# The third group's work on k and its first use of q, moved from ahead of a gate product to behind it

## The chip, the cores and the metric

The kernel runs on one core of a Trainium2 chip. The metric is the device time of one execution in microseconds (us). TensorE (PE in the profile), VectorE (DVE), ScalarE (ACT) and GpSimd (POOL) each work through their own list of instructions in order and wait for each other by semaphores; SyncE (SP) issues the transfers.

## What is computed

Three stages follow each other on 8 batches of 576 tokens (4608 in all), 8 heads of 64 features:

```
q_s = softmax(q) over the 64 features of a head
k_s = softmax(k) over the 576 tokens of a batch
kv  = k_s^T v          # 64 x 64 per head
x   = q_s kv           # the attention's output, 512 features a token
xn  = x / rms(x) * rms_g
y   = (silu(xn w_gate) * (xn w_val)) w_out
z   = max(y w1, y w2, y w3) w_out2
```

Everything is float32 at the ends. The large products run as three matmuls on a high and a low part of each factor.

## The kernel before

The tokens are cut into nine **groups** of 512, g = 0 to 8. Groups 0 to 7 are the first 512 tokens of each batch, group 8 is the 64 left over of all eight. The work of the attention on one group falls into four **pairs of heads**, p = 0 to 3, and names carry both: k_2_0 is k of group 2 (the third), pair 0.

The first part of the kernel, up to about 620 us, is a loop `iteration(g, nxt, f)` over nine groups and f = 0 to 11, twelve blocks of 128 hidden features of the gated layer. Each call computes a **gate product** pg (twelve matmuls of 128x512, lines 640 to 642), ScalarE's tanh of it into t (L1003), VectorE's product with it (L1004), a **value product** pv (twelve more matmuls) and h (L1025). Between them stands the attention of a later group, spread over the calls so that TensorE need not stop. Even f and odd f make one *turn*; `turn_of` gives each target (g, p) a turn, and `due(n)` lists the targets whose turn is n turns ahead. For a target of group 2 or later the steps are:

- two turns ahead: k's columns come in, `k_max` takes the maximum per feature (km, L455), `q_exp` takes q's maximum and exponential by token (qm, L417; q, L429 and L430), and q's sums follow (L382 to L385). The statistics of q go to DRAM and come back as broadcasts (`spread_stats`, the tile stat).
- one turn ahead, odd f: `k_exp`. TensorE spreads km over the partitions by a transposition into the bank pb (L477), VectorE subtracts it from k (L478), ScalarE takes the exponential (L479).
- in its turn, even f, behind the gate product: `make_kv`. TensorE multiplies k and v into pk (L488, five matmuls in ten records); VectorE divides (L492 to L501) and the result is split into kvh and kvl.
- in its turn: `q_softmax` on the transposed q (qT: POOL L390, ACT L391, POOL L392), then `q_by_feature` (qh, ql).
- later: `make_x`. TensorE multiplies q and kv into px (L534 to L536), ScalarE copies it (xraw, L546) and squares it (sq, L552), GpSimd adds the squares up (sacc, L554). For group 2 this comes one turn later, at the head of an even f; for later groups two turns later.

When a group's four x are there, `token_rstd` sums the squares on TensorE (L590: pv of sacc or whole), and at the group's end the x are scaled (L622) and split into a high and a low part (ACT L99, DVE L100: xh, xl or x), which the next group's first gate product reads.

Beside this, ScalarE, VectorE and GpSimd recode the weights of the second layer (st, rooms_o, L247 to L274).

What is written here is not the order on the engines. The framework's scheduler places every instruction of each engine anew from the code's order and its dependencies, so that one moved call also moves neighbours that the diff does not name. TensorE's instructions stand in the order of its list, and one that waits holds back all behind it; the same goes for the other engines.

## Time and profile before

| | |
|---|---|
| median of 3 runs | 1506.61 us (1505.65 to 1508.04) |
| the profiled execution | 1505.86 us |
| its span, first to last instruction | 1504.1 us |
| TensorE busy | 1481.2 us, 98% of the span |
| VectorE busy | 1058.3 us, 70% |
| ScalarE busy | 607.1 us, 40% |
| GpSimd busy | 455.5 us, 30% |
| TensorE in the chain that ended last | 67% of the span; VectorE 3%, DMA 2% |

TensorE is the busiest by far, and its waits are few, so the profile is read by looking for the places where TensorE's list stood still. A row of the timeline gives the start of an instruction, its duration, engine, line, operation and tiles, and in brackets how long the engine had been idle and what ended that. Matmuls overlap: one follows the next after 0.23 us although each lasts 0.39 us. So time lost is read from start to start, and the idle time in brackets is less than what was lost.

### The profile page before, as it was taken

Reading aid. Unit: us, or ns where it says so; the run is one execution under the profiler, and the core shown is the slowest. Engines: PE = TensorE matmul, PEld = TensorE weight load, DVE = VectorE, ACT = ScalarE, POOL = GpSimd, SP = SyncE. Lnnn points to the kernel's source line nnn. Section 1 sums busy time; section 2 is a strip of 40 time slices with the busy share of each in tenths; the row PEclk is TensorE's granted clock in tenths of the full one; section 3 lists DMA queues with packets and bytes.
Section 4 is the critical chain, followed back from the end, with each engine's and each line's share of the span. In section 5 each row is a group of like instructions: output and inputs, shape, how many; then the busy total and the mean of one; then the engine's idle time right before and its main releaser. Section 6 shows DMA issues by size and latency. Waiting matters only on the chain.

```text
span 1504.1 us, 19788 instructions
## 1 busy us (share of the span) xinstructions
PE 1481.2 (98%) x6724; PEld 1215.4 (81%) x6724; DVE 1058.3 (70%) x1761; ACT 607.1 (40%) x1158; POOL 455.5 (30%) x383
## 2 busy tenths in 40 slices
PE   8899999999999999999999999999999999999998
PEld 5677878788888888888888888888888888888887
DVE  7998686867587864463798989658748748747622
ACT  6764443435343444332545545422422423413311
POOL 1002444444444444251365765111111111111100
PEclk9999999999999999999999999999999999999999
DMA  6868998878888968679535335265585585585572
GB/s 221 274 192 217 259 261 244 274 223 250 241 267 239 270 186 270 213 255 331 190 131 207 116 126 196 85 234 192 214 291 189 202 292 196 192 279 190 187 260 98
DMA packets 158757, 329.12 MB, mean 219 GB/s; under 512 B 31040, under 2 KB 55616, under 8 KB 158656
## 3 DMA queue, kind: packets, MB, share of 16 engines
q1 hardware_dynamic: 155200, 321.56, 66.4%
q10 hardware_dynamic: 3456, 6.29, 1.1%
q8 instruction: 53, 0.87, 0.2%
q14 instruction: 48, 0.39, 0.1%
HBM read 245.24 MB, written 82.55 MB: 218 GB/s over the span
## 4 chain that ended last, share of the span: by engine, by line
PE 67%; DVE 3%; DMA 2%; issue 1%; POOL 0%; ACT 0%; SPq 0%; DVEq 0%; ACTq 0%
PE p_a L647 4%; PE p_a L646 4%; PE p_a L648 4%; PE o_acc L647 4%; PE o_acc L646 4%; PE o_acc L648 4%; PE pv L642 3%; PE pv L640 3%; PE pv L641 3%; PE pg L640 3%; PE pg L641 3%; PE pg L642 3%; PE p_G L646 2%; PE p_G L647 2%; PE p_G L648 2%; PE o_a L646 2%
## 5 line engine op out<-in xcount | busy, mean ns | idle before, releaser
L1119 POOL TENSOR_TENSOR temps_wl<-temps_wl,temps_wh 128x512 f32<-128x512 f32 x36 | 48.2, 1339 | 348.5 <-ACT temps_wh L1118 273.8
L274 POOL TENSOR_TENSOR rooms_o<-st,rooms_o 128x256 fp32r<-128x256 f32 x77 | 62.6, 823 | 110.2 <-ACT rooms_o L273 99.7
L1004 DVE SCALAR_TENSOR_TENSOR t<-t,pg 128x512 f32<-128x512 f32 x64 | 43.8, 684 | 71.2 <-ACT t L1003 71.2
L1110 DVE TENSOR_TENSOR temps_wl<-temps_wl,p_a 128x512 f32<-128x512 f32 x72 | 49.2, 683 | 37.3 <-POOL temps_wl L1119 37.1
L429 POOL TENSOR_TENSOR q<-q,qm 128x512 f32<-128x512 f32 x30 | 34.3, 1145 | 135.5 <-DVE kr L494 82.2
L1114 ACT COPY temps_wh<-p_G 128x512 f32<-128x512 f32 x36 | 21.1, 586 | 106.0 <-PE p_G L648 105.8
L648 PE MATMUL p_a<-x_wh,chunk 128*128 128x512 f32 x160 | 62.3, 389 | 0.0
L647 PE MATMUL p_a<-x_wl,chunk 128*128 128x512 f32 x160 | 62.3, 389 | 0.0
L646 PE MATMUL p_a<-x_wh,chunk 128*128 128x512 f32 x160 | 62.3, 389 | 0.0
L646 PE MATMUL p_a<-x_wl,chunk 128*128 128x512 f32 x160 | 62.3, 389 | 0.0
L647 PE MATMUL p_a<-x_wh,chunk 128*128 128x512 f32 x160 | 62.3, 389 | 0.0
L648 PE MATMUL p_a<-x_wl,chunk 128*128 128x512 f32 x160 | 62.3, 389 | 0.0
L1025 DVE SCALAR_TENSOR_TENSOR h<-t,pv 128x512 f32<-128x512 f32 x66 | 45.2, 685 | 20.2 <-PE pv L642 18.4
L1116 DVE TENSOR_TENSOR temps_wl<-temps_wh,p_V 128x512 f32<-128x512 f32 x36 | 24.6, 684 | 43.9 <-PE p_V L648 43.9
L1003 ACT ACTIVATE t<-pg 128x512 f32<-128x512 f32 x64 | 37.8, 591 | 42.0 <-PE pg L642 38.3
L805 POOL TENSOR_TENSOR h_X<-h_Y,h_X 128x512 f32<-128x512 f32 x24 | 40.2, 1684 | 38.7 <-DVE o_xl L100 21.6
L809 POOL TENSOR_TENSOR h_Z<-h_Z,h_X 128x512 f32<-128x512 f32 x24 | 39.8, 1676 | 38.1 <-DVE h_X L802 34.2
L273 ACT CAST rooms_o<-st 128x256 fp32r<-128x256 f32 x77 | 31.5, 424 | 41.2 <-DMA w_dram<-rooms_o 21.6
L1004 DVE SCALAR_TENSOR_TENSOR rooms_o<-rooms_o,pg 128x512 f32<-128x512 f32 x42 | 28.7, 682 | 25.3 <-ACT rooms_o L1003 25.2
L807 POOL TENSOR_TENSOR h_Y<-h_W,h_Y 128x512 f32<-128x512 f32 x24 | 38.7, 1620 | 13.6 <-DMA h_W<-h_dram 12.9
L274 POOL TENSOR_TENSOR rooms_o<-rooms_o,rooms_o 128x256 fp32r<-128x256 f32 x36 | 28.8, 808 | 44.5 <-ACT rooms_o L273 36.8
L488 PEld LDWEIGHTS pk<-v,k 128*128 128x128 f32 x300 | 37.9, 190 | 5.0 <-ACT k L479 3.1
(1256 smaller groups left out, 4990.0 us busy)
## 6 DMA issues: line engine op xcount, KB each, us to landing
chunk<-w_dram SPq DMA_DIRECT2D x112, 768.0 KB, 4.4
w_dram<-rooms_o SPq DMA_DIRECT2D x113, 256.0 KB, 4.3
h_dram<-h SPq DMA_DIRECT2D x108, 256.0 KB, 4.2
stat<-stats SPq DMA_DIRECT2D x112, 128.0 KB, 5.1
words<-in_w SPq DMA_DIRECT2D x24, 512.0 KB, 6.9
chunk<-w_dram SPq DMA_DIRECT2D x48, 256.0 KB, 3.5
k<-in_k SPq DMA_DIRECT2D x30, 320.0 KB, 4.6
v<-in_v SPq DMA_DIRECT2D x30, 320.0 KB, 5.7
```

The source lines that it names most:

```text
L274: nc.gpsimd.tensor_sub(t[:, 1, :], src, t[:, 0, :].bitcast(F32))
L640: nc.tensor.matmul(pt, hi[:, j, s], xhs[kk], start=(kk == 0), stop=False)
L641: nc.tensor.matmul(pt, hi[:, j, s], xls[kk], start=False, stop=False)
L642: nc.tensor.matmul(pt, lo[:, j, s], xhs[kk], start=False, stop=(kk == 3))
L646: nc.tensor.matmul(pt, ah, bh, start=first, stop=False, skip_group_check=onto)
L647: nc.tensor.matmul(pt, ah, bl, start=False, stop=False, skip_group_check=onto)
L648: nc.tensor.matmul(pt, al, bh, start=False, stop=last, skip_group_check=onto)
L805: nc.gpsimd.tensor_sub(x, y, x)
L1004: nc.vector.scalar_tensor_tensor(t, t, 1.0, pg, op0=ALU.add, op1=ALU.mult)
L1025: lows.append(nc.vector.scalar_tensor_tensor(h, t, 0.5, pv, op0=ALU.mult, op1=ALU.mult))
L1110: nc.vector.tensor_add(y, x, pt)
L1119: nc.gpsimd.tensor_add(w, u2, s5)
```

## The change

Two steps are moved inside `iteration`. For targets of group 2 and later, `k_exp` no longer stands ahead of the odd gate product but behind it and its tanh. For targets of group 2, `make_x` no longer stands ahead of the even gate product but behind it, just ahead of `make_kv`. Nothing is added, nothing removed: 24 calls of `k_exp` and 4 of `make_x` move. (Group 8 has no k of its own, and group 1 has its own calls, which stay.)

```diff
@@ -941,8 +941,6 @@
             for t in due(-1):
                 if t[0] > BY_FEATURE:
                     q_by_feature(*t)
-                else:
-                    make_x(*t)
             for t in due(0):
                 q_softmax(*t)
             for t in due(1):
@@ -966,8 +964,6 @@
                     for t in due(2):
                         k_max(*t)
                         q_stats(*t)
-            for t in due(1):
-                k_exp(*t)
             for t in due(0):
                 if t[0] == BY_FEATURE:
                     q_by_feature(*t)
@@ -1003,8 +999,14 @@
         nc.scalar.activation(t, pg, AF.Tanh, scale=0.5)
         nc.vector.scalar_tensor_tensor(t, t, 1.0, pg, op0=ALU.add, op1=ALU.mult)
         if not odd:
+            for item in due(-1):
+                if item[0] == BY_FEATURE:
+                    make_x(*item)
             for item in due(0):
                 make_kv(*item)
+        else:
+            for item in due(1):
+                k_exp(*item)
         if nxt == BY_FEATURE and f == 10:
             spread_rstd(nxt)
             for p in range(4):
```

On TensorE the built program differs in just these moves and one more. All 24 transpositions of km stand behind the twelve matmuls of the gate product, and px of the third group behind the even gate product. SyncE's list is the same to the last row. On VectorE, ScalarE and GpSimd the neighbours of the moved instructions change places too. Three places matter below. In the changed kernel lines from 1003 on have numbers two to four away: the tanh is L999 there, the product with it L1000, h L1027.

The first place is the change from the first group to the second (g = 1, f = 0). ScalarE's list there, before:

```order
L99 CAST x_1_2_1396<-xraw_1_3_1223 128x512
L479 ACTIVATE k_2_0_1229<-k_2_0_1229 128x640
L391 ACTIVATE qT_2_0_1304<-qT_2_0_1304 128x512
L1003 ACTIVATE t_1_0_1460<-pg_1_0_1447 128x512
L99 CAST qh_2_0_1521<-qT_2_0_1304 128x512
```

And in the changed kernel:

```order
L99 CAST x_1_2_1392<-xraw_1_3_1223 128x512
L391 ACTIVATE qT_2_0_1304<-qT_2_0_1304 128x512
L479 ACTIVATE k_2_0_1229<-k_2_0_1229 128x640
L999 ACTIVATE t_1_0_1460<-pg_1_0_1447 128x512
L99 CAST qh_2_0_1517<-qT_2_0_1304 128x512
```

The exponential of k for (2, 0) has moved behind that of the transposed q of the same target. TensorE's list there in the changed kernel, from the last matmul of the gate product:

```order
L642 MATMUL pg_1_0_1447<-x_1_2_1392,wl_(1, 0)_519 128x512
L640 MATMUL pv_1_0_1479<-x_1_0_1384,wh_(1, 0)_516 128x512
L641 MATMUL pv_1_0_1479<-x_1_0_1384,wh_(1, 0)_516 128x512
L642 MATMUL pv_1_0_1479<-x_1_0_1384,wl_(1, 0)_519 128x512
L488 MATMUL pk_2_0_1463<-v_0_0_219,k_2_0_1229 128x129 x5
L640 MATMUL pv_1_0_1479<-x_1_0_1384,wh_(1, 0)_516 128x512
```

Before, pk of (2, 0) stood right behind the gate product; now three matmuls of the value product stand ahead of it.

The second place is the last x of the third group (g = 1, f = 8). ScalarE before:

```order
L546 ACTIVATE xraw_2_3_1980<-px_2_3_1976,gain_214 128x512
L552 ACTIVATE sq_2_3_1982<-px_2_3_1976 128x512
L273 CAST rooms_o5_1430<-rooms_o7_1432 128x256
L1003 ACTIVATE t_1_8_2011<-pg_1_8_1998 128x512
L430 ACTIVATE q_3_2_1858<-q_3_2_1858 128x512
L247 ACTIVATE st2_4_1911<-st2_4_1911 128x512
```

And in the changed kernel:

```order
L273 CAST rooms_o5_1430<-rooms_o7_1432 128x256
L999 ACTIVATE t_1_8_2002<-pg_1_8_1989 128x512
L546 ACTIVATE xraw_2_3_2009<-px_2_3_2005,gain_214 128x512
L430 ACTIVATE q_3_2_1849<-q_3_2_1849 128x512
L552 ACTIVATE sq_2_3_2011<-px_2_3_2005 128x512
L247 ACTIVATE st2_4_1911<-st2_4_1911 128x512
```

The last square of the group, which the sum of squares needs, has moved behind an exponential of q. On GpSimd the addition of it (L554) has moved in the same way behind the subtraction that this exponential waits for (L429).

The third place is VectorE's list at (6, 2), g = 4, f = 11. Before:

```order
L382 TENSOR_REDUCE qs_6_3_4490<-q_6_3_4277 128x8
L478 TENSOR_TENSOR k_6_2_4343<-k_6_2_4343,pb_6_2_4495 128x640
L383 TENSOR_SCALAR qs_6_3_4490<-qs_6_3_4490 128x8
L248 TENSOR_SCALAR st2_19_4392<-st2_19_4392 128x512
L385 RECIPROCAL qr_6_3_4493<-qs_6_3_4490 128x8
L249 SCALAR_TENSOR_TENSOR st2_19_4392<-st2_19_4392 128x512
L261 TENSOR_TENSOR st2_19_4392<-st2_19_4392 128x256
L1004 SCALAR_TENSOR_TENSOR rooms_o6_1431<-rooms_o6_1431,pg_4_11_4510 128x512
```

And in the changed kernel:

```order
L382 TENSOR_REDUCE qs_6_3_4490<-q_6_3_4277 128x8
L383 TENSOR_SCALAR qs_6_3_4490<-qs_6_3_4490 128x8
L248 TENSOR_SCALAR st2_19_4392<-st2_19_4392 128x512
L385 RECIPROCAL qr_6_3_4493<-qs_6_3_4490 128x8
L249 SCALAR_TENSOR_TENSOR st2_19_4392<-st2_19_4392 128x512
L261 TENSOR_TENSOR st2_19_4392<-st2_19_4392 128x256
L478 TENSOR_TENSOR k_6_2_4343<-k_6_2_4343,pb_6_2_4521 128x640
L1000 SCALAR_TENSOR_TENSOR rooms_o6_1431<-rooms_o6_1431,pg_4_11_4506 128x512
```

The subtraction from k stands five instructions later. At the change to the next group, (2, 0), (3, 2) and (7, 2), it stands behind the four splits of x (L100) and, there too, behind the product with the tanh.

## Rows read from the trace of the kernel before

**Rows 1.** The page: busy time by engine; TensorE's granted clock in 40 slices.

```profile
PE 1481.2 (98%) x6724; PEld 1215.4 (81%) x6724; DVE 1058.3 (70%) x1761; ACT 607.1 (40%) x1158; POOL 455.5 (30%) x383
...
PEclk9999999999999999999999999999999999999999
```

**Rows 2.** Timeline, TensorE, first gate product of the second group (start, duration, instruction, [idle]).

```profile
120.87 0.39 PE L640 MATMUL pg<-x,wh_(1, 0)_516 128*128 128x512 f32 x1
121.96 0.50 PE L641 MATMUL pg<-x,wh_(1, 0)_516 128*128 128x512 f32 x1 [0.70 <-DVE x L100]
...
124.62 1.28 PE L488 MATMUL pk<-v,k 128*128 128x129 f32 x10
```

**Rows 3.** Timeline there, GpSimd and ScalarE.

```profile
124.95 1.27 POOL L390 TENSOR_TENSOR qT<-qT,stat 128x512 f32<-128x512 f32 x1 [13.20 <-DMA stat<-stats]
...
126.25 0.63 ACT L391 ACTIVATE qT<-qT 128x512 f32<-128x512 f32 x1 [4.26 <-POOL qT L390]
126.79 0.58 ACT L1003 ACTIVATE t<-pg 128x512 f32<-128x512 f32 x1
```

**Rows 4.** Timeline, TensorE, px of (2, 1).

```profile
146.77 0.39 PE L642 MATMUL pv<-x,wl_(1, 3)_770 128*128 128x512 f32 x1
147.96 0.49 PE L534 MATMUL px<-qh,kvh 128*128 128x512 f32 x1 [0.80 <-ACT qh L99]
...
149.25 0.39 PE L640 MATMUL pg<-x,wh_(1, 4)_815 128*128 128x512 f32 x1
```

**Rows 5.** Timeline, ScalarE, GpSimd, TensorE, around the last square of the third group.

```profile
177.63 0.59 ACT L552 ACTIVATE sq<-px 128x512 f32<-128x512 f32 x1
...
181.38 0.63 ACT L430 ACTIVATE q<-q 128x512 f32<-128x512 f32 x1 [2.35 <-POOL q L429]
181.92 0.65 ACT L247 ACTIVATE st<-st 128x512 f32<-128x512 f32 x1
...
178.36 1.29 POOL L554 TENSOR_TENSOR sacc<-sacc,sq 128x512 f32<-128x512 f32 x1 [0.34 <-ACT sq L552]
...
181.81 0.84 PE L590 MATMUL pv<-ones_f,sacc 128*128 128x1 f32 x7
```

**Rows 6.** Timeline, TensorE, first gate product of the third group, from its first matmul to pk.

```profile
201.82 0.40 PE L640 MATMUL pg<-xh,wh_(1, 0)_516 128*128 128x512 f32 x1
...
205.71 0.50 PE L488 MATMUL pk<-v,k 128*128 128x129 f32 x3
```

**Rows 7.** Timeline, TensorE, transposition of km of (4, 3), and what stands ahead of it.

```profile
283.67 0.39 PE L642 MATMUL pv<-x,wl_(1, 0)_519 128*128 128x512 f32 x1
285.49 0.30 PE L477 MATMUL pb<-ident,km 128*128 128x128 f32 x1 [1.43 <-DVE km L455]
```

**Rows 8.** Timeline, TensorE, sum of squares of the sixth group.

```profile
396.73 0.49 PE L590 MATMUL pv<-ones_f,whole 128*128 128x1 f32 x3 [0.52 <-POOL whole L558]
```

**Rows 9.** Timeline, VectorE, ScalarE, TensorE, around k of (6, 2).

```profile
429.00 0.81 DVE L478 TENSOR_TENSOR k<-k,pb 128x640 f32<-128x640 f32 x1
429.72 0.17 DVE L383 TENSOR_SCALAR qs<-qs 128x8 f32<-128x8 f32 x1
...
431.39 0.68 DVE L1004 SCALAR_TENSOR_TENSOR rooms_o<-rooms_o,pg 128x512 f32<-128x512 f32 x1
...
429.90 0.74 ACT L479 ACTIVATE k<-k 128x640 f32<-128x640 f32 x1 [2.18 <-DVE qs L383]
...
429.68 0.39 PE L640 MATMUL pg<-x,wh_(1, 0)_516 128*128 128x512 f32 x1
...
431.04 0.83 PE L488 MATMUL pk<-v,k 128*128 128x129 f32 x6
```

**Rows 10.** Timeline, TensorE and VectorE, around k of (7, 2).

```profile
504.66 0.39 PE L640 MATMUL pg<-xh,wh_(1, 0)_516 128*128 128x512 f32 x1
...
506.09 0.61 PE L488 MATMUL pk<-v,k 128*128 128x129 f32 x4
...
505.39 0.67 DVE L1004 SCALAR_TENSOR_TENSOR rooms_o<-rooms_o,pg 128x512 f32<-128x512 f32 x1
```

## The prediction

> **What bounds the kernel now.** The page comes first: TensorE is busy 98% of the span, the next engine 70% [rows 1]. So the time is the length of TensorE's list plus the places where it stands still, and the change adds no instruction to any list. The timeline of TensorE comes next, read from start to start in the part that the change touches (115 to 575 us). Undisturbed, six matmuls of 512 columns take 1.36 us, from 429.68 to 431.04, so one follows the next after 0.23 us [rows 9]; three of them cost 0.69, twelve 2.74. Every start that is later than that is lost. Then the other engines' timelines show what came late. In this part the list stands still for half a microsecond or more at only six places [rows 2, 4, 6, 7, 8 and 10]. They are the first gate products of three groups, where a split of x is late; px of (2, 1), where qh and ql are late; one transposition of km; and one sum of squares.
>
> **What the moves take away.** I call the sum of what is gained and lost so far the *shift*; TensorE carries it to the end, for it is the bound in all that follows.
>
> 1. px of (2, 1). From the last matmul of a product at 146.77 to the first of the next at 149.25, four steps that should take 0.92 took 2.48 [rows 4]: 1.55 lost, on ScalarE's qh and then VectorE's ql. Behind the gate product px comes 2.74 later, and both are there. **-1.55.** The other three px had no such wait.
> 2. The transposition of km for (4, 3) came 1.82 after the matmul before it, instead of 0.23, because km was late [rows 7]. Behind the gate product it comes 2.74 later and km is there. **-1.6.**
> 3. Where the third group begins, the twelve matmuls of the gate product took from 201.82 to 205.71, 3.89 for 2.74 [rows 6]: 1.15 lost on the splits of x, which had stood behind the subtraction from k on VectorE. That subtraction (0.81 [rows 9]) now stands behind the splits. The splits come earlier and TensorE later, so this goes. In its place pk of (3, 2) may wait, for its subtraction now comes last. By rows that are not this late it waits for nothing; at most it takes 0.8 back. I take 0.1: **-1.0** (-1.1 to -0.3).
>
> **What the moves put in their place.** Four things are new or larger.
>
> 4. (2, 0), where the second group begins. On ScalarE the exponential of k now stands behind that of qT. That one started at 126.25 because it waited for GpSimd, which had been idle 13.2 us until the broadcast of the statistics landed [rows 3]. The transfers' list is the same, so it starts then again. The next on ScalarE began at 126.79; k's exponential, 0.74 long [rows 9], then ends at 127.53. TensorE follows a late input after 0.05 (the split that began at 121.22 and ended at 121.91 let it start at 121.96 [rows 2]), and a matmul after a wait costs 0.1 more (that product took 3.75 from 120.87 to pk at 124.62, 1.0 over, of which 0.86 before the late matmul and the rest behind it [rows 2]). So pk begins at 127.58 and is 0.1 longer. Before it began at 124.62, with three matmuls fewer ahead of it (0.69), which are no loss: 127.68 - 124.62 - 0.69 = **+2.4**. The wait for x at 121.96 goes, but that is in this number: TensorE just stands about 3.3 us at pk instead.
> 5. The last square of the third group now stands on ScalarE behind the exponential of q for (3, 2), which began at 181.38 and let the next start at 181.92 [rows 5]. With the square's 0.59 it ends at 182.51, GpSimd starts 0.14 later (178.36 after a square that ended at 178.22) and adds for 1.29: 183.94, and the sum of squares on TensorE begins at 183.99. TensorE comes there at 181.81, less 0.1 for the transposition that now stands behind, plus a shift of 2.4 - 1.55 = 0.85, so at 182.56. The wait is 1.4 and the 0.1 behind it. That is the low end. q's exponential hangs on q's maximum on VectorE, which stands behind h and now behind the moved subtraction of (3, 0), and h is released by TensorE; if that chain moves with the shift it is 2.4. I take **+2.3**, near the high end, because the subtraction is in that chain as well.
> 6. (6, 2). k's exponential ended at 430.64, 0.40 before TensorE came to pk at 431.04 [rows 9]. The subtraction moves behind the five instructions that took from 429.72 to 431.39, 1.67 in all [rows 9]. So the exponential ends at 432.31 and pk starts at 432.36, 1.32 late, and 0.1 behind it: **+1.4**. If VectorE does not move with the shift, as little as 0.9.
> 7. (7, 2). The splits lost TensorE 0.74 (1.43 for three steps of 0.23 [rows 10]). They come earlier, and the subtraction stands behind them and behind the product with the tanh. That product began at 505.39 [rows 10]; without the subtraction ahead of it 0.72 earlier, at 504.67, for the next instruction on VectorE starts 0.72 after a subtraction of 0.81, 0.09 before its end [rows 9]. By the same 0.09 the subtraction follows the product (0.67 long) after 0.58. It ends at 506.06, the exponential some 0.8 later, and pk starts at 506.9 instead of 506.09, with 0.1 behind it: **+0.9**. If VectorE lags less than the shift, the whole wait is hidden and the place gains 0.7.
> 8. The sum of squares of the sixth group waits for GpSimd at 396.73 [rows 8]. The transposition ahead of it, 0.1, lay within that wait and now stands behind it, and GpSimd moves a little with the shift: **+0.25** (0.1 to 0.4).
>
> The other 20 calls of k's step and three of x's cost nothing that I can price: TensorE did not wait for their results, and the move takes 2.74 of TensorE's time and a few instructions of VectorE's. That cover is thinner after the change, and it is a rival below.
>
> **The sum**: -1.55 - 1.6 - 1.0 + 2.4 + 2.3 + 1.4 + 0.9 + 0.25 = +3.1. The profiled execution took 1505.86; with the change I expect 1509.0. The median of the runs is 0.75 above the profiled one, so the median I expect is **1509.7**, 0.2% above 1506.61. With all low ends the sum is about 0, with all high ends 4.2. A measurement of this kernel tells about 0.2%, 3.0 us, from no change, so my forecast lies on that line.
>
> **The rivals.**
> - *Not slower: ScalarE and VectorE arrive in time.* Steps 5, 6 and 7 all hang on one thing, how far VectorE and ScalarE lag behind TensorE. If they come to the moved instruction some 1.5 us earlier against TensorE than these rows say, which they would if they do not share the shift, those waits close. Then 2.3, 1.4 and 1.6 go from the sum: -2.2, a median of 1504.4. For it: the products with the tanh and the splits lose the subtraction ahead of them. Against it: it takes all three at once, and at (6, 2) only 0.40 was left [rows 9].
> - *More waits at pk.* The move uses up most of the cover of other products of k and v. Two of them coming 0.6 late give 4.3 and a median of 1510.9. For it: VectorE is at 70% and the lag grows with what stands ahead. Against it: at no other place does the subtraction move behind as much as at a group's end.
> - *TensorE's clock falls at the new wait.* The granted clock stayed at its full level all through, beside waits on TensorE of up to 1.4 us in the part in question [rows 1, 7]; at (2, 0) there would be one of 3.3. At the lower level (1.2 of 2.4 GHz) a step would take 0.46 instead of 0.23; for the nine matmuls left of that product that is 2.1 more, a median of 1511.8. The Trainium skill bears on it (TensorE: Matmul & The Clock Gate, section Why this matters for your kernels): it advises against pauses of TensorE between bursts of matmuls, because an idle stretch can bring the clock back to half. The rows here have no wait as long as the new one, so they neither bear it out nor deny it.
>
> That the change does not do what it says is no rival: the order of the built program shows it.
>
> **How the numbers follow.** The forecast, 0 to +4.2, has 0.74; it lies on both sides of the line, 0.36 within 0.2% and 0.38 above. The first rival has 0.12, half of it beyond 0.2%, if the other low ends come too, and half within. More waits have 0.08 and the clock 0.06, all slower by more. That makes 0.06 faster, 0.42 the same, 0.52 slower. The range reaches from 1506.4, a little under the forecast's low end, to 1512.2, over the last two rivals' prices; below it lies most of the first rival.
>
> **What would show it.** The timeline of TensorE at the first gate product of the second group: pk some 3.3 us late with ScalarE's k named, and no wait for x at the starts of the second, third and seventh groups. px of (2, 1) and the transposition of (4, 3) without idle time. The sum of squares at g = 1, f = 9 late with GpSimd's sacc named, some 2.3. pk of (6, 2) and (7, 2) 1.3 to 1.6 late. I am wrong if pk of (2, 0) starts without a wait (then step 4 falls and the sum is below 1), or if the waits taken away come back at the same matmuls.

## The result and the profile after

The changed kernel took 1513.3 us (median of 6 runs, 1511.17 to 1514.97) where the kernel before took 1505.87 (6 runs, 1502.68 to 1508.04): a ratio of 1.0053, with a 95% interval of 1.0042 to 1.0064. The profiled execution took 1511.17, its span 1509.4. So it is slower, and by more than the range of the prediction allowed: of the 7.4 us the forecast had 3.1.

The page first, against [rows 1]: TensorE's busy time rose by 2.6 us though it has the same list, and the span by 5.3. Of the 2.6, 1.2 lie ahead of 115 us, where TensorE's list is the same: there the granted clock was at half from 48.6 to 52.0.

```profile
span 1509.4 us, 19787 instructions
...
PE 1483.8 (98%) x6724; PEld 1218.1 (81%) x6724; DVE 1061.8 (70%) x1761; ACT 609.0 (40%) x1158; POOL 455.3 (30%) x383
```

The same chain as in [rows 2] and [rows 3]: the timeline of TensorE at the second group's first products, then of GpSimd and ScalarE there.

```profile
124.12 0.39 PE L642 MATMUL pv<-x,wl_(1, 0)_519 128*128 128x512 f32 x1
127.07 2.52 PE L488 MATMUL pk<-v,k 128*128 128x129 f32 x10 [2.56 <-ACT k L479]
...
131.99 0.39 PE L640 MATMUL pg<-x,wh_(1, 1)_581 128*128 128x512 f32 x1
...
124.46 1.27 POOL L390 TENSOR_TENSOR qT<-qT,stat 128x512 f32<-128x512 f32 x1 [13.10 <-DMA stat<-stats]
...
125.76 0.63 ACT L391 ACTIVATE qT<-qT 128x512 f32<-128x512 f32 x1 [5.01 <-POOL qT L390]
126.30 0.72 ACT L479 ACTIVATE k<-k 128x640 f32<-128x640 f32 x1
```

This is the new wait as forecast: k's exponential starts when that of qT lets it, and pk follows it. pk starts 2.95 after the matmul ahead of it, 2.72 late; forecast were 3.3, the broadcast landed 0.5 sooner. But pk's ten records now last 2.52 where the kernel before needed 1.28 [rows 2]. The table by stretches says why (columns: stretch, its length, busy time of PE, PEld, DVE, ACT and POOL, then the granted clock, DMA share, GB/s):

```profile
126.00:128.00 2.00, 0.93 (x4) 0.94 (x5) 0.47 (x1) 1.73 (x4) 1.53 (x2) 0.77 0.32 86
128.00:130.00 2.00, 2.00 (x10) 1.91 (x9) 1.41 (x4) 1.02 (x2) 0.74 (x1) 0.50 0.61 149
130.00:132.00 2.00, 2.00 (x10) 1.60 (x9) 0.86 (x3) 0.30 (x1) 0.00 (x0) 0.87 1.03 377
132.00:134.00 2.00, 2.00 (x10) 1.68 (x9) 1.81 (x3) 0.00 (x0) 0.00 (x0) 1.00 1.04 424
```

From about 127.1 to 130.5 TensorE ran at the lower of its two levels, 1.2 instead of 2.4 GHz. The whole place, from the first gate matmul to the first of the next gate product, took 11.47 us (120.52 to 131.99), against 7.66 before (120.87 to 128.53): 3.81 more. From pk to the next gate product an undisturbed list needs 3.23 (before, 124.62 to 128.53, less three matmuls of 0.23); here it took 4.92. So 1.69 of the 3.81 is the clock, and 2.12 the wait.

px of (2, 1) and the transposition of (4, 3), [rows 4] and [rows 7], now come without idle time (timeline of TensorE):

```profile
153.16 0.40 PE L534 MATMUL px<-qh,kvh 128*128 128x512 f32 x1
...
292.18 0.39 PE L642 MATMUL pg<-x,wl_(1, 1)_601 128*128 128x512 f32 x1
292.40 0.27 PE L477 MATMUL pb<-ident,km 128*128 128x128 f32 x1
```

The sum of squares of the third group, [rows 5]: TensorE, then ScalarE, then GpSimd.

```profile
183.23 0.39 PE L642 MATMUL pv<-x,wl_(1, 8)_1135 128*128 128x512 f32 x1
185.84 1.05 PE L590 MATMUL pv<-ones_f,sacc 128*128 128x1 f32 x8 [2.22 <-POOL sacc L554]
...
183.25 0.63 ACT L430 ACTIVATE q<-q 128x512 f32<-128x512 f32 x1 [1.43 <-POOL q L429]
183.79 0.58 ACT L552 ACTIVATE sq<-px 128x512 f32<-128x512 f32 x1
...
184.51 1.27 POOL L554 TENSOR_TENSOR sacc<-sacc,sq 128x512 f32<-128x512 f32 x1 [1.29 <-ACT sq L552]
```

As forecast, the square stands behind q's exponential, and the sum is 2.4 late. The third group's start, [rows 6], is what went against the forecast (TensorE, VectorE, ScalarE):

```profile
205.77 0.39 PE L640 MATMUL pg<-xh,wh_(1, 0)_516 128*128 128x512 f32 x1
...
208.41 0.50 PE L641 MATMUL pg<-xl,wh_(1, 0)_516 128*128 128x512 f32 x1 [0.16 <-DVE xl L100]
208.74 0.40 PE L642 MATMUL pg<-xh,wl_(1, 0)_519 128*128 128x512 f32 x1
210.50 1.38 PE L488 MATMUL pk<-v,k 128*128 128x129 f32 x10 [1.37 <-ACT k L479]
...
208.28 0.68 DVE L1000 SCALAR_TENSOR_TENSOR rooms_o<-rooms_o,pg 128x512 f32<-128x512 f32 x1
208.88 0.81 DVE L478 TENSOR_TENSOR k<-k,pb 128x640 f32<-128x640 f32 x1
...
209.72 0.74 ACT L479 ACTIVATE k<-k 128x640 f32<-128x640 f32 x1 [4.74 <-DVE k L478]
```

The gate product is slowed by little, 0.33 at 208.41, but pk waits 1.53 for product, subtraction and exponential one after the other. The remaining places, [rows 8 to 10] and two more (TensorE):

```profile
285.71 0.49 PE L488 MATMUL pk<-v,k 128*128 128x129 f32 x2 [0.56 <-ACT k L479]
...
400.88 1.05 PE L590 MATMUL pv<-ones_f,whole 128*128 128x1 f32 x8 [0.22 <-POOL whole L558]
...
436.90 1.38 PE L488 MATMUL pk<-v,k 128*128 128x129 f32 x10 [1.41 <-ACT k L479]
...
511.34 1.28 PE L488 MATMUL pk<-v,k 128*128 128x129 f32 x10
```

pk of (4, 2) waits, which the sum did not have (it was a rival); pk of (6, 2) waits 1.57, as forecast; pk of (7, 2) does not wait, against the forecast.

*Lateness* below is how much later the same product begins than in the first trace of the kernel before, and a place's price is how much the lateness grows across it. Every variant below has the trace of one execution, which can lie some us from its median. The first trace of the changed kernel gives:

| place | forecast | measured |
|---|---|---|
| ahead of 120 us | 0 | -0.35 |
| start of the second group, (2,0) | +2.4 | +3.81 |
| px of (2,1) | -1.55 | -1.60 |
| sum of squares, third group | +2.3 | +2.35 |
| start of the third group, (3,2) | -1.0 | +0.95 |
| pk of (4,2), then transposition of (4,3) | 0, -1.6 | +0.83, -1.67 |
| pk of (5,2) | 0 | +0.35 |
| sum of squares, sixth group | +0.25 | -0.27 |
| (6,2) | +1.4 | +1.61 |
| (7,2) | +0.9 | -0.74 |
| rest | 0 | 0 |
| sum | +3.1 | +5.3 |

### The profile page after: what moved, and what is told of

The parts are those of the page before. It is cut to its first block, busy times and chain, and to the rows that moved or that the text cites. A ratio compares the mean times of both kernels' runs of the same rounds, so it can differ in the third digit from the quotient of the medians.

```text
span 1509.4 us, 19787 instructions
## 1 busy us (share of the span) xinstructions
PE 1483.8 (98%) x6724; PEld 1218.1 (81%) x6724; DVE 1061.8 (70%) x1761; ACT 609.0 (40%) x1158; POOL 455.3 (30%) x383
## 4 chain that ended last, share of the span: by engine, by line
PE 66%; DVE 5%; DMA 2%; issue 1%; POOL 1%; ACT 1%; SPq 0%; DVEq 0%; POOLq 0%; ACTq 0%
PE p_a L646 4%; PE p_a L648 4%; PE p_a L647 4%; PE o_acc L648 3%; PE o_acc L647 3%; PE o_acc L646 3%; PE pv L642 3%; PE pv L640 3%; PE pv L641 3%; PE pg L640 3%; PE pg L641 3%; PE pg L642 3%; PE p_G L646 2%; PE p_G L648 2%; PE p_G L647 2%; PE o_a L646 2%
## 5 line engine op out<-in xcount | busy, mean ns | idle before, releaser
L274 POOL TENSOR_TENSOR rooms_o<-st,rooms_o 128x256 fp32r<-128x256 f32 x77 | 62.5, 820 | 116.4 <-ACT rooms_o L273 101.8
L1000 DVE SCALAR_TENSOR_TENSOR t<-t,pg 128x512 f32<-128x512 f32 x64 | 43.8, 685 | 72.7 <-ACT t L999 72.5
L429 POOL TENSOR_TENSOR q<-q,qm 128x512 f32<-128x512 f32 x30 | 34.6, 1154 | 134.6 <-DVE kr L494 81.7
L1027 DVE SCALAR_TENSOR_TENSOR h<-t,pv 128x512 f32<-128x512 f32 x66 | 45.2, 685 | 19.6 <-PE pv L642 18.0
L999 ACT ACTIVATE t<-pg 128x512 f32<-128x512 f32 x64 | 37.9, 592 | 42.8 <-PE pg L642 37.6
L488 PE MATMUL pk<-v,k 128*128 128x129 f32 x300 | 41.5, 286 | 8.0 <-ACT k L479 7.9
L999 ACT ACTIVATE rooms_o<-pg 128x512 f32<-128x512 f32 x42 | 24.9, 593 | 52.9 <-PE pg L642 52.8
L274 POOL TENSOR_TENSOR rooms_o<-rooms_o,rooms_o 128x256 fp32r<-128x256 f32 x36 | 28.9, 811 | 49.9 <-ACT rooms_o L273 47.6
```

The lines of the kernel that those rows point to most:

```text
L274: nc.gpsimd.tensor_sub(t[:, 1, :], src, t[:, 0, :].bitcast(F32))
L488: nc.tensor.matmul(pk[:, 0 : P + 1], k_t[g, p][:, c, :], v_t[g, p][:, c, :], start=(c == 0), stop=(c == 4))
L999: nc.scalar.activation(t, pg, AF.Tanh, scale=0.5)
L1027: lows.append(nc.vector.scalar_tensor_tensor(h, t, 0.5, pv, op0=ALU.mult, op1=ALU.mult))
```

## The experiments

**The theory** at the start: the waits are where the forecast put them, the lower clock behind the longest adds 1.7, and each place's price stands by itself. **The rivals**: that the clock does not hang on the wait; and that waits are not added up but passed on, since what comes late hangs on broadcasts, GpSimd and VectorE rather than on TensorE, so that time saved at one place is waited for at the next.

Most variants use the same edit, which lets one choose the calls that move. The changed kernel has all 24 in the first list and all four of group 2 in the second.

```diff
+            for t in due(1):
+                if t not in K_BEHIND:
+                    k_exp(*t)
...
             for item in due(1):
-                k_exp(*item)
+                if item in K_BEHIND:
+                    k_exp(*item)
```

and the same for `make_x` with X_BEHIND. Each variant ran beside the kernel before on the same chip, and each ratio is to that; chips differ, the medians of the kernel before were 1508.8 to 1509.5 on these.

### The changed kernel once more

> The changed kernel once more. Theory (waits plus clock): TensorE stands some 2.6 us at the product with k of (2, 0) and the granted clock falls to 0.5 behind it, which makes the second group's start 3.8 us longer than before; the time is 1511 to 1515, 0.5% above before. The executions of the changed kernel that took up to 3.8 us longer than its profiled one have further stretches at the lower clock, behind the 2.2 us wait for the sum of squares or in the first stage near 49 us. Rival: the clock is at half in no second place of the later stages, and the spread of executions comes from the first stage alone (before 115 us), as it does in the kernel before.

1518.57 us (5 runs, 1517.91 to 1519.91), the kernel before 1509.53 (17 runs): 1.0060 (1.0043 to 1.0078). The timeline of GpSimd and of TensorE, and the granted clock (columns as above) at (2,0) and at (6,2):

```profile
126.66 1.26 POOL L390 TENSOR_TENSOR qT<-qT,stat 128x512 f32<-128x512 f32 x1 [14.26 <-DMA stat<-stats]
...
129.27 0.49 PE L488 MATMUL pk<-v,k 128*128 128x129 f32 x2 [4.15 <-ACT k L479]
...
440.60 2.52 PE L488 MATMUL pk<-v,k 128*128 128x129 f32 x10 [2.28 <-ACT k L479]
...
130.00:132.00 2.00, 2.00 (x9) 1.86 (x9) 1.73 (x5) 1.22 (x2) 0.94 (x1) 0.50 1.01 343
440.00:442.00 2.00, 1.40 (x6) 1.40 (x7) 2.00 (x6) 1.42 (x4) 0.31 (x1) 0.58 1.04 376
442.00:444.00 2.00, 2.00 (x10) 1.76 (x8) 1.14 (x2) 2.00 (x5) 1.13 (x2) 0.56 0.98 204
```

The broadcast landed 5.1 after the gate product's start (121.56) instead of 3.9, and the wait at (2,0) is 4.15 instead of 2.56: that place costs 4.95 here. (6,2) costs 3.98 instead of 1.61, half clock included, (7,2) costs +0.84, near the forecast's +0.9, and pk of (6,1) 0.97. So the rival, that no second place of the later stages has the lower clock, is wrong: (6,2) has one. The places of the theory, the sum of squares or the first stage, are not those of this trace: its first stage shows full clock. The first trace of the changed kernel was at the fast end of what the kernel does; this one shows where the rest of the 7.4 can lie, but the other executions have no trace.

### One part alone

> Only k's step is moved; x's products stay ahead of the gate products. Theory: the second group's start loses 3.8 as in the changed kernel (2.1 wait, 1.7 clock); the sum of squares of the third group is not late, because its last square is ahead of q's exponential again (0 instead of +2.35); the third group's start, (4,3), (5,2), (6,2) and (7,2) are as in the changed kernel (+1.0, -0.85, +0.35, +1.7, -0.75 and -0.3 for the sixth group's sum of squares); px of (2,1) waits 1.55 as before: in all +5.0, 1511 us. Rival: the new shift of 3.8 covers the wait at px of (2,1) as well, since its inputs hang on a broadcast that is not late: +3.4, 1509.

```diff
+    K_BEHIND = [(g, p) for g in range(2, 8) for p in range(4)]
+    X_BEHIND = []
```

1517.97 (1.0052, 1.0035 to 1.0069). The lateness, 0.97 at the second group's start, grew by 4.0 there, and px of (2,1) gained 1.55 although x is not moved: the rival on that point is right. The sum of squares is not late (-0.1), as expected. But the third group's start cost 3.3 where 1.0 was expected: the gate product now waits at all four splits (2.36 in all), and pk another 1.54. The total, 8.4 us above the kernel before, is past both expectations and cannot be told from the changed kernel's on this chip, 1518.57: leaving x's products where they were saved nothing.

> Only x's product of the third group is moved; k's step stays ahead of the gate products. Theory: px of (2,1) loses its wait (-1.6) and the sum of squares of the third group is 2.3 late, because its last square stands behind q's exponential: +0.7, 1506.6 us, and no stretch at the lower clock at the second group's start. Rival: the sum of squares is late only as far as the second group's start is (the chain hangs on TensorE): then 1.4 here and -0.2 in all, 1505.7.

```diff
+    K_BEHIND = []
+    X_BEHIND = [(2, 0), (2, 1), (2, 2), (2, 3)]
```

1511.73 (11 runs; 1.0014, 1.0002 to 1.0025). px gained 1.60, the sum of squares waited 2.60 for GpSimd, and the clock was at half from 182.9 to 189.7: the place cost 5.8. The third group's start then gained 1.15, for TensorE came so late that x was there. Both expectations had the sum of squares right in kind and too small, and neither had a fall of the clock.

### The clock or the wait

> The changed kernel with eleven matmuls of 512 columns more (2.5 us, their result is overwritten) on TensorE ahead of the product with k of (2, 0), where it stands idle 2.6 us. Theory (the idle time lets the clock fall): no stretch at 0.5 near 127 to 131 us, the product with k starts at the same time as without them, and the next gate product begins 1.7 us earlier: 1.8 instead of 3.5 later than in the kernel before; the whole 1.7 shorter than the changed kernel, some 1511.6 where that takes 1513.3. Rival (the idle time is not the cause; it is the transfers or the place in the program): the clock falls all the same and the gate product begins 3.5 later.

```diff
+            if g == 1 and f == 0:
+                pv = bank("V", f"pv_{g}_{f}")
+                for _ in range(11):
+                    nc.tensor.matmul(pv, wh[wkey][:, 1, 0:P], xhs[0], start=True, stop=True)
+                third = product_in(pv, wh[wkey], wl[wkey], 1, xhs, xls, 0, 1)
+                with tc.issue_after(third.ins):
+                    for item in due(0):
+                        make_kv(*item)
+                product_in(pv, wh[wkey], wl[wkey], 1, xhs, xls, 1, 4)
```

The timeline of TensorE and its granted clock at (2,0):

```profile
126.94 1.38 PE L488 MATMUL pk<-v,k 128*128 128x129 f32 x10 [0.35 <-ACT k L479]
...
126.00:128.00 2.00, 1.65 (x12) 1.22 (x11) 0.59 (x1) 1.73 (x4) 1.66 (x2) 1.00 0.22 36
128.00:130.00 2.00, 2.00 (x11) 1.67 (x11) 1.71 (x6) 0.90 (x2) 0.62 (x1) 1.00 0.70 188
```

pk starts when k's exponential lets it, as without the fill, and the clock stays at full level; from pk to the next gate product 3.29 instead of 4.92. That is the price of the clock again, 1.63: the idle time is the cause there, and the rival falls (one trace with the fill, against six without it in which the clock fell here). The next gate product begins 1.70 later than in the first trace of the kernel before (1.8 expected), of which 1.23 had been gained ahead of the place; the place costs 2.93, against 3.81 and 4.95 in the two traces of the changed kernel. The whole did not get shorter, though: 1520.49 (1.0071, 1.0053 to 1.0088). The eleven instructions made the scheduler place others differently in the second group, and TensorE waited 2.57 at 167.5 and 3.84 at 186.2 for k's exponential, there with the lower clock from 182.8 to 189.6. As a test of the total it says nothing, as one of the place it does.

### Taking single places back

> The kernel before once more, for a second trace of it beside those of the other variants. Theory (the places of the waits belong to the order of the instructions, their sizes partly to when the statistics' broadcasts land): TensorE stands still at the same six places as in the first trace, each within 0.7 us of it, no stretch at the lower clock between 100 and 620 us, and a time within 0.3% of 1506. Rival (the chip's state makes the waits): waits at other places, or a stretch at half clock between 100 and 620 us.

1507.99 us. Only three of the six places lose half a microsecond or more as before: the starts of the second and third groups, and the sum of squares of the sixth group, which waited 1.07 instead of 0.56. px of (2,1) lost 0.74 instead of 1.55, the transposition of (4,3) 0.30 instead of 1.59, the seventh group's start 0.22 instead of 0.74; the transposition of (3,2) waited 0.85 instead of 0.27. And the clock was at half from 400.0 to 403.4 without any change to the kernel, which cost 1.6: here the rival is right. So part of the waits and of the clock belongs to the single execution, and one trace against one trace tells a place's price to about 1.3 us, a fall of the clock apart.

> The changed kernel, but k's step of (2,0) stays where it was. Theory: the wait at the product with k of (2,0) and the half clock behind it go (-3.8 to -5), the wait for x at 121 comes back inside that; of the rest the sum of squares of the third group stays late, by more than in the changed kernel since TensorE comes earlier: +3.5 on before, ratio 1.0023. Rival: all later waits hang on broadcasts and not on TensorE, so what is saved is waited for at the sum of squares and at (3,2) and (6,2): ratio 1.005, as the changed kernel.

```diff
+    K_BEHIND = [(g, p) for g in range(2, 8) for p in range(4) if (g, p) != (2, 0)]
```

1519.77 (6 runs; 1.0074, 1.0057 to 1.0091): no gain at all. The wait at (2,0) and the fall of the clock at 127 are gone, and the lateness at 128.5 is 0.01. Then, in the timeline of TensorE, the next three pk and the sum of squares wait:

```profile
151.27 1.38 PE L490 MATMUL pk<-v,k 128*128 128x129 f32 x10 [0.70 <-ACT k L481]
...
165.96 1.38 PE L490 MATMUL pk<-v,k 128*128 128x129 f32 x10 [1.53 <-ACT k L481]
...
179.91 1.38 PE L490 MATMUL pk<-v,k 128*128 128x129 f32 x10 [0.79 <-ACT k L481]
...
186.74 1.05 PE L592 MATMUL pv<-ones_f,sacc 128*128 128x1 f32 x8 [2.70 <-POOL sacc L556]
```

With the lower clock from 189.0 to 192.5 the lateness is 6.8 at 194.9, more than in either trace of the changed kernel (4.3 and 6.0). The rival is right: the wait at (2,0) had covered these.

> The changed kernel, but x's product of (2,3) stays ahead of the gate product, so that its square stands ahead of q's exponential on ScalarE. Theory: the sum of squares of the third group is not late: 2.3 less than the changed kernel, ratio 1.004 on before; the third group's start is unchanged (its splits and k's subtraction hang on VectorE). Rival: the sum of squares waits all the same, since what makes it late is the shift of 3.8 ahead of it: ratio 1.0055.

```diff
+    X_BEHIND = [(2, 0), (2, 1), (2, 2)]
```

1518.24 (6 runs; 1.0070, 1.0053 to 1.0087). The last square stands ahead of q's exponential again, and the sum of squares is on time (+0.2): step 5 of the prediction named the right cause. The 2.35 are not saved, however. The gate product of the third group, reached sooner, waits 2.3 for the four splits and pk 1.54, with the lower clock behind it: 4.8 there instead of 0.95. The first of the splits and pk (TensorE; lines have other numbers here):

```profile
205.36 0.50 PE L643 MATMUL pg<-xl,wh_(1, 0)_516 128*128 128x512 f32 x1 [0.50 <-DVE xl L100]
...
211.52 0.98 PE L490 MATMUL pk<-v,k 128*128 128x129 f32 x6 [1.37 <-ACT k L481]
```

Theory and rival were both wrong on the total: the wait went, and moved on.

> The changed kernel, but k's step of (3,2), (4,2), (5,2), (6,2) and (7,2), the five that stand at a group's start, stays where it was. Theory (each of these stands on VectorE behind the splits and the product with the tanh, and TensorE waits for it at the product with k): their waits go, 5 to 7 us together in the traces of the changed kernel; what is left is the second group's start (+4 to +5), px of (2,1) (-1.6), the sum of squares (+2) and (4,3) (-1.65): +3.5, ratio 1.0023. Rival: waits saved at one place are waited for at the next, as where k's step of (2,0) was put back: ratio 1.005 to 1.006.

```diff
+    K_BEHIND = [(g, p) for g in range(2, 8) for p in range(4) if p != 2 or g == 2]
```

1513.08 (12 runs; 1.0021, 1.0008 to 1.0035), as the theory said; the rival's 1.005 is outside. The five pk at the groups' starts no longer wait; the third group's start gains 1.15, as in the variant with x alone. (2,0) cost 5.84 in this trace, with the clock at half from 128.5 to 135.3.

> The kernel before with k's step moved for (3,2), (4,2), (5,2), (6,2) and (7,2) alone. Theory: pk of these stands still as in the changed kernel: +1.0 to +1.5 at (3,2), 0.3 to 1 at (5,2), 1.7 to 4 at (6,2), -0.7 to 1.5 at (7,2): +5, ratio 1.0035, and these five make most of what the changed kernel loses. Rival: they cost only together with the rest: below +2, ratio under 1.0013.

```diff
+    K_BEHIND = [(g, 2) for g in (3, 4, 5, 6, 7)]
+    X_BEHIND = []
```

1514.36 (11 runs; 1.0029, 1.0018 to 1.0039): five calls of 24 make half of the loss, near the theory's 1.0035. Prices: 3.8 at (3,2), 0.8 at (4,2), 0.7 at (5,2), 1.9 at (6,2), 0.6 at (7,2); the transposition of (4,3) still gained 1.6, since TensorE came to it later.

> The kernel before with k's step of (2,0) moved alone. Theory: TensorE stands 2.5 to 4.3 us at its product with k, the granted clock falls to half behind it, and the next gate product begins 4 to 5 us late; then the wait for px of (2,1) (1.55) and a part of the third group's start (1.15) vanish in this lateness, since their inputs do not hang on TensorE: +2.5 in all, ratio 1.0016. Rival: later waits hang on TensorE and the whole stays: +4.5, ratio 1.003.

```diff
+    K_BEHIND = [(2, 0)]
+    X_BEHIND = []
```

1512.12 (12 runs; 1.0015, 1.0002 to 1.0028), the theory's value. The place cost 3.73 (the wait, and the lower clock from 128.1 to 131.5); then px of (2,1) lost its wait (-1.55) and the third group's start 0.85, though neither was touched.

> The kernel before with x's product moved for (2,0), (2,1) and (2,2), not for (2,3). Theory: px of (2,1) without its wait (-1.55), the last square ahead of q's exponential and so the sum of squares not late: -1.55, ratio 0.999; the loss of the variant that moves all four is the last one's alone. Rival: the sum of squares waits as in that variant (+3.6 and more), since it is the chain ahead of the square that is late: ratio 1.001.

```diff
+    K_BEHIND = []
+    X_BEHIND = [(2, 0), (2, 1), (2, 2)]
```

1509.69 against 1509.21 (12 runs; 0.9999, 0.9988 to 1.0011). px of (2,1) gained 1.60 and the sum of squares is on time, so the loss of the variant with all four x is the last one's. But at 198 the transposition of km of (3,2) waited 2.2 for the bank that it shares with the spread of the third group's statistics (TensorE):

```profile
198.12 0.32 PE L479 MATMUL pb<-ident,km 128*128 128x128 f32 x1 [2.01 <-ACT rooms_o L620]
```

In this trace the gain is gone behind it; the interval still holds the theory's 0.999.

> Only two calls are moved: k's step of (4,3) and x's product of (2,1), the two at whose own instruction TensorE stood still before and that gained in every trace so far. Theory: the wait at px of (2,1) goes (-1.55) and the one at the transposition of (4,3) (-1.65), nothing takes their place: -3.2 us, ratio 0.9979. Rival: TensorE, 1.55 earlier, then waits as much longer for the third group's x, whose sum of squares stands behind the same chain: -1.65 only, ratio 0.999.

```diff
+    K_BEHIND = [(4, 3)]
+    X_BEHIND = [(2, 1)]
```

1507.03 (12 runs, 1503.53 to 1513.18) against 1508.77 (17 runs, 1505.27 to 1512.99): 0.9990, 0.9976 to 1.0004. This is the lowest ratio of all variants, at the rival's value, but the interval holds the theory's 0.9979 and no change as well. In its trace, which is that of the slowest execution, the transposition at 198 waits 2.3, as in the last variant, and the sum of squares of the sixth group 3.5.

### Why the third group's start did not gain

The term that was furthest off was the third group's start: the subtraction, 0.81, was taken away from ahead of the splits, and they ended no sooner.

> The kernel before with k's step of (3,2) moved alone. Theory (VectorE and GpSimd hold each other up): without the subtraction in between, VectorE's first split of x starts ahead of GpSimd's multiplication of q, which then takes 1.8 us instead of 1.3, and VectorE's short instruction behind the split (0.17 by itself) lasts until that ends, 1.2 to 1.3; so the last split ends no sooner than in the kernel before, counted from the product of x with its statistics, the gate product loses as much or more, and TensorE stands 1.3 to 1.5 more at pk: +1.5 to +3.8 at this place. Rival (VectorE's list alone counts): the splits end 0.8 sooner and the place costs nothing or gains, unless the sum of squares is late as well.

> As the one that moves (3,2) alone, but GpSimd's multiplication of q's exponential by the reciprocals is left out for (3,1), so that nothing of GpSimd's lies beside the first splits. Theory: VectorE's short instruction takes 0.17 instead of 1.26, the splits end some 1.1 sooner (less if GpSimd's additions move up and hold them instead), the wait at pk shrinks by as much. Rival: the short instruction waits for something else (its sums): it lasts as long as before.

> As the one that moves (3,2) alone, but the same multiplication for (3,1) is done by VectorE, between the second split and the third. Theory: VectorE has 0.7 more to do and is not held 1.1: the splits end some 0.4 sooner. Rival: VectorE is the bound by its own list, and they end 0.7 later.

> The kernel before without GpSimd's multiplication for (3,1), nothing moved. Theory: the multiplication lay beside the subtraction from k and held VectorE only at its end (0.64 for 0.17), so the splits end 0.5 sooner and the loss of 1.15 at the gate product shrinks to some 0.7. Rival: VectorE was not held at all, and nothing changes.

```diff
+    K_BEHIND = [(3, 2)]
...
-        nc.gpsimd.tensor_mul(qT[g, p], qT[g, p], r)
+        if (g, p) != (3, 1):
+            nc.gpsimd.tensor_mul(qT[g, p], qT[g, p], r)
```

(The last three lines are the edit of the two that leave the multiplication out; the one on VectorE has the line below instead. The second kernel without it is the kernel before with nothing moved.)

```diff
+        (nc.vector if (g, p) == (3, 1) else nc.gpsimd).tensor_mul(qT[g, p], qT[g, p], r)
```

The kernel before, second trace: VectorE from q's sums to the splits, and GpSimd's multiplication.

```profile
201.92 0.68 DVE L382 TENSOR_REDUCE qs<-q 128x8 f32<-128x512 f32 x1
202.51 0.81 DVE L478 TENSOR_TENSOR k<-k,pb 128x640 f32<-128x640 f32 x1
203.24 0.64 DVE L383 TENSOR_SCALAR qs<-qs 128x8 f32<-128x8 f32 x1
...
204.51 2.39 DVE L100 TENSOR_TENSOR xl<-xraw,xh 128x512 fp32r<-128x512 f32 x3
...
202.54 1.30 POOL L392 TENSOR_TENSOR rooms_o<-rooms_o,stat 128x512 f32<-128x512 f32 x1 [1.81 <-ACT rooms_o L391]
```

The same with (3,2) moved:

```profile
202.56 0.68 DVE L382 TENSOR_REDUCE qs<-q 128x8 f32<-128x512 f32 x1
203.16 0.68 DVE L100 TENSOR_TENSOR xl<-xraw,xh 128x512 fp32r<-128x512 f32 x1
203.76 1.26 DVE L383 TENSOR_SCALAR qs<-qs 128x8 f32<-128x8 f32 x1
...
205.65 2.26 DVE L100 TENSOR_TENSOR xl<-xraw,xh 128x512 fp32r<-128x512 f32 x2
...
203.19 1.79 POOL L392 TENSOR_TENSOR rooms_o<-rooms_o,stat 128x512 f32<-128x512 f32 x1 [2.42 <-ACT rooms_o L391]
```

And with (3,2) moved and the multiplication left out:

```profile
200.59 0.68 DVE L382 TENSOR_REDUCE qs<-q 128x8 f32<-128x512 f32 x1
...
201.79 0.16 DVE L383 TENSOR_SCALAR qs<-qs 128x8 f32<-128x8 f32 x1
...
202.57 2.27 DVE L100 TENSOR_TENSOR xl<-xraw,xh 128x512 fp32r<-128x512 f32 x2
```

L383 adds a constant to 8 columns and takes 0.16 by itself. Beside GpSimd's multiplication it ends 0.03 after that does, in both traces, and with the multiplication left out it takes 0.16 there too: it is held. In the kernel before, the subtraction ran beside the multiplication and neither slowed the other (0.81 and 1.30). Moved away, the first split takes its place, holds up the multiplication (1.79 instead of 1.30), and then L383 is held for 1.1. From the start of L382 to the end of the last split it takes 4.98 before, 5.35 with (3,2) moved, 4.25 with the multiplication left out, and 4.51 in the kernel before without it. So the two engines hold each other, 1.10 with the move and 0.47 without, as the theory expected (1.1 and 0.5). The Trainium skill states the rule (SBUF — State Buffer, section Who interferes with whom): the two engines share a pair of ports; a VectorE instruction with two inputs in SBUF and a GpSimd instruction that reads SBUF exclude each other, and whichever comes first holds the ports to its end. A VectorE instruction with at most one SBUF input does not contend, by the same section, unless it runs in a mode that uses both ports, which a `tensor_scalar`, as L383 is, can enter. The rows agree: the subtraction takes its second input from the PSUM bank pb, the split takes both from SBUF, and L383, with one, was held; no row shows its mode.

That is not the whole hold. The last two splits take 2.27 with the multiplication left out as well, where two that nothing holds take 1.28 (0.60 from start to start, and 0.68); GpSimd's additions L274 lie beside them. In the kernel before only the last split is so long (1.23, the one ahead of it 0.68). This is read from the rows; no variant took these additions away. So with the multiplication gone in both, the move shortens the stretch by 0.26 (4.51 to 4.25) and not by the subtraction's 0.8.

With the multiplication on VectorE the same stretch takes 5.40, not 0.4 less: it needed 1.25 instead of 0.68 there, because GpSimd's additions for the second layer's weights (L274) had moved up beside it. That expectation fell, and so did its rival's 0.7 later. And in all three variants with (3,2) moved pk waits 1.53 to 1.54: leaving the multiplication out ends the splits sooner but does not touch the chain behind the last one, so the wait at pk did not shrink, as had been expected; the loss of the whole place did, from 3.8 to 2.2. (With (3,2) alone moved the clock fell too, from 210.7 to 214.1, which cost 1.1 more behind it.) In the kernel before without the multiplication the gate product lost nothing at all where 0.7 was expected; TensorE came there 2.5 later, so that part was not tested. The four single runs took 1514.5, 1508.53, 1513.16 and 1508.92, the kernel before 1510.5.

## Why the prediction was wrong, step by step

The median, 1513.3, lies above the range, and the traced execution was 2.2 us past the forecast's sum. Three misses, 4.8 together, stand behind that: step 3 had the wrong sign (+1.95 against its term), the clock behind the wait of step 4 stood in the sum at nothing (+1.69), and so did more waits at pk (+1.18). That the sum came as near as 2.2 is luck: above all, (7,2) gave 0.74 where 0.9 was forecast as a loss.

**Steps 1 and 2** (px of (2,1), transposition of (4,3)) were right to 0.1 in the first trace of the changed kernel, and in the second, against the first trace of the kernel before. Against its second trace they are worth 0.8 and 0.4: the waits that they take away were themselves smaller there. What they did not say is that px's wait also goes when anything ahead makes TensorE late, as k's step of (2,0) alone does.

**Step 3** (start of the third group) is the term of wrong sign, +0.95 for -1.0, and +1.5 in the second trace of the changed kernel. Two parts failed. That the splits come earlier by the subtraction's 0.81 overlooked that this time was shared with GpSimd. Only 0.33 of the 1.15 was left at the gate product in the first trace, but that was because TensorE had already waited 2.35 at the sum of squares. Where it had not (k's step alone, or all but the last x), the gate product waited longer than before. And "at most 0.8" for pk counted the subtraction alone. Behind the last split stand the product with the tanh, the subtraction and the exponential, 0.60, 0.84 and 0.78 from start to start, and TensorE has two steps to do meanwhile: pk waited 1.53 or 1.54 in eight of the ten traces that have (3,2) moved.

**Step 4** (start of the second group) had the wait, its cause and its rows right, and its size to 0.3: +2.1 for +2.4. The missing 1.7 is the clock. The rival had the mechanism and the price (2.1 for nine matmuls; measured 1.69 and 1.63) but a chance of 0.06, and that was the worst single judgement: it weighed that the rows had no fall, and they had no wait of that length from which to learn it. In all six traces with k's step of (2,0) moved and no fill, the clock fell here, within the wait or at most 0.5 us after it, at idle times of 2.56 to 4.15. That agrees in kind with the advice of the Trainium skill that the prediction cited (TensorE: Matmul & The Clock Gate, section Why this matters for your kernels). The size of the wait itself hangs on when the broadcast lands, and that differs from execution to execution (below).

**Step 5** (sum of squares) was right in size and cause, +2.35 for +2.3, and the variant without the last x shows the cause. But it was not worth 2.3: without it the third group waits instead.

**Steps 6, 7, 8**: +1.61 for +1.4, -0.74 for +0.9, -0.27 for +0.25 in the first trace; +3.98, +0.84 and +0.29 in the second. Step 7 took its low end in one trace and its middle in the other. The cover that step 6 read from one trace, 0.40, was 1.55 in the second trace of the kernel before. The first rival, that these waits close, did not come true but at (7,2).

**The rival of more waits at pk** came true as well: (4,2) and (5,2), +0.8 and +0.35, had 2.2 of cover in the kernel before (k's exponential ended that long ahead of pk), and the move takes more from the pair 2 of a group than from others; that this is because the splits of a group's four x stand there on VectorE fits the order but was tried at (3,2) alone.

**The method** failed in one thing beside the terms: it added places. The variants show that places in a row can share one lateness. Taking the wait at (2,0) away gained nothing, taking the sum of squares away gained nothing, and x's gain at (2,1) was waited for at 198. What fits these is the later of two, TensorE's own list and the chain that makes the input. From the second group's start to the third group's value product the lateness grew by 5.3 and 6.5 in the two traces of the changed kernel, by 5.9 with k's step alone, and by 5.8 and 6.4 where (2,0) or the last x had been put back; in the second trace of the kernel before it grew by 0.7. It does not hold everywhere: putting the groups' starts back did lower the time, to 1.0021. (Its trace has 6.4 in the same stretch, but 5.84 of that fell at (2,0), ahead of what was put back.) At (2,0) the chain starts at a broadcast that GpSimd waits for. The third group's splits start from TensorE's own sum of squares, so their chain moves with TensorE; what delays it beyond that was tried on VectorE and GpSimd alone.

**What stays open** is how the 7.4 us of the six runs divide, since only one of them has a trace, with 5.3; the second trace of the changed kernel shows the broadcast 1.2 later against TensorE and a second fall of the clock. The traces show where that 1.2 arises: in all 18, of whichever kernel, SyncE issues the first of the four broadcasts 3.1 to 3.2 us ahead of the second group's gate product, and GpSimd can start 3.5 to 5.3 after its start. So the broadcasts move with TensorE, and what differs is the transfers' own time; why it differs was not tried.

## What to carry to other kernels

When a step is moved behind cover, compute each place anew as the later of the bound engine's arrival and the chain of work that makes its input (at (2,0) from a broadcast), instead of adding differences place by place: a wait taken away early is often waited for later. Before counting an instruction's time as gained by its engine, look what ran beside it on the engine that shares its ports; an instruction that contends with nothing may have been free where it stood. And where a change makes the bound engine stand longer than anywhere in the old trace, its clock must be in the sum and not among the small chances.

## What the runs showed of the chip that was not expected

The lower clock is less rare than the first trace of the kernel before says. In its second trace TensorE ran at half from 48.5 to 55.3, in the first stage, and from 400.0 to 403.4, where the wait ahead, ended at 397.73, had been 1.02; in the changed kernel an idle time of 2.22, ended at 185.84, had no fall behind it. So the length of one wait alone does not tell in these traces. The stretch at half clock from 127.1 to 130.5 cost 1.7 us of TensorE's work, the one from 182.9 to 189.7 (x's products alone moved) 3.2, which is the place's 5.8 less the wait of 2.6.

An instruction of VectorE on 8 columns (L383) took 0.16 to 0.17 us alone and up to 1.27 where GpSimd had a multiplication under way, ending 0.03 after it.
